# One PSUM tile of two banks for the scores and the up-projections, a quarter of K on GpSimd, and another place for weight splits and the last steps of attention

## The chip, the cores and the metric

The kernel runs on one core of one Trainium2 chip. The metric is the device time of the whole program in microseconds. The engines are called PE (TensorE), DVE (VectorE), ACT (ScalarE), POOL (GpSimd) and SP (SyncE, which issues most transfers). PSUM, the memory that PE writes to, is used here as eight banks of 128 partitions by 512 float32 values.

## The reference

The inputs are `r`, `k`, `v`, `w` of 4 batches, 8 heads, 768 steps and 48 channels, and a mixture of 8 experts (384 to 1024 to 384 channels). First comes a linear attention with a decaying state, then each of the 3072 rows goes through one expert.

```python
for t in range(S):
    cur = np.einsum('bhd,bhe->bhde', u[None] * kt, vt)
    y[:, :, t] = np.einsum('bhd,bhde->bhe', rt, state + cur)
    state = wt[:, :, :, None] * state + np.einsum('bhd,bhe->bhde', kt, vt)
...
logits = x @ w_gate + modality_bias[modality_id]
e_idx = np.argmax(logits, axis=1)
...
for e in range(E):
    h = np.maximum(x[mask] @ w1[e], 0.0)
    out[mask] = gate_w[mask, None] * (h @ w2[e])
```

`gate_w` is the softmax value of the chosen expert.

## The kernel before

The framework runs each engine's instructions in the order in which the code issues them (`manual_schedule`, line 55). It adds the semaphore waits by itself, from which instruction reads and writes which tile. All pools of PSUM have one buffer for a tag, so a tag is a fixed place, and a new tile of a tag waits for the readers of the old one.

**Attention** works on 24 chunks of 128 steps (4 batches of 6 chunks), all heads at once. `att_iter(i)`, for i from -2 to 23, does a third of the work of each of three chunks: it prepares chunk a = i+2, makes scores for m = i+1, and makes the output of z = i.

- Preparing: DVE makes the products of the decays by two scans, `B` (L251) and `E` (L254), and then `R = r*E` (L215) and `K = k*B` (L221). ACT first copies r and k to the PSUM tile `pX` (L211), from which `mk_r` and `mk_k` read. POOL makes `G = r*k` (L256), after the scan `E` by a dependency that the code adds.
- Scores: PE transposes the four 128-wide quarters of K into `pK` (L283), which ACT copies to `KT`, and makes the scores of four head pairs: even heads go to tile `pS0`, odd heads to `pS1`, 512 wide each (L301). DVE multiplies each by the mask into `A` (L303), two operations of 512.
- State: PE adds K^T v into `pU` (L310), ACT scales it to `SP` and copies it into `SPb`.
- Output: PE makes `pY` from R and `SPb` (L331) and from A and v (L337). POOL makes `dV` (L262), the term with `u`; DVE adds the two to `xp` (L361, `x_rows`) one iteration later. One iteration after that PE transposes these rows (L368, `x_cols`), ACT copies them to `xT`, and PE makes the router's logits in the tile `pR` (L374, `logits`).

**Routing** of the first 12 chunks runs inside the loop, as "hooks": `route_a` at i = 14, `route_b` at 15, `table(0)` at 16. All three are mostly small DVE operations. POOL then scatters the rows to their sorted places in DRAM by indirect transfers (L555), two of them at i = 15, three at each of 16 to 18 and one at 19.

**The experts** follow in blocks of 256 rows, 12 of them here, and one half block of 128 rows. Products are made to nearly float32 precision by splitting each operand into a rounded part and a rest: `wh`, `wl` for weights, `xh`, `xo` for rows, `hh`, `hl` for hidden values. A weight split (`w_split`) is a copy on ACT (L206) and a subtraction (L207) on DVE for w1 and on POOL for w2. `blk_up(q, g)` for g = 0 to 3 makes two 128-wide parts of the hidden layer by 18 matmuls (L596) into one PSUM tile of 2 by 256, which takes the tags `pS0`, `pS1`, `pT` in turn. ACT reads it for `hh` (L601), DVE reads it and `hh` for `hl` (L602). `blk_down` (L613) multiplies by w2 into `pY` and `pX`; ACT scales the result and POOL scatters it. `half_up` is the half block's `blk_up`, two groups in `pS0` and `pS1`. In block 0, `x_cols` and `logits` of the last two chunks stand between the groups of `blk_up`, in the tag `pT`.

The first expert's w1 is split during attention, in eight parts of 384 columns, at the iterations that `SPLITS` lists (line 240), on POOL behind `dV`. The bias table of the router is put together early in POOL's queue, with a scratch area `bt2` (line 158) in the space that the raw weights take later.

Of the kernel before, what the change touches and what calls it, by code (L numbers as in the profile page):

```python
# [52 lines left out]
def kernel(ctx: ExitStack, tc: tile.TileContext, rkw, vt, wf, cst, mid, wg, bias, w1, w2, out):  # L53
# [150 lines left out]
    def w_split(k, q, n=2, eng=None):  # L204
        sl = slice(n * q, n * q + n)
        nc.scalar.copy(out=wh[k][:, sl], in_=raw[k][:, sl])  # L206
        (eng or (nc.vector, nc.gpsimd)[k]).tensor_tensor(out=wl[k][:, sl], in0=raw[k][:, sl], in1=wh[k][:, sl].bitcast(F32), op=ALU.subtract)  # L207
# [9 lines left out]
    def mk_k(a):  # L217

        kk = T["pX", a] if a else ins[0][:, 512:1024].rearrange("p (a b) -> p a b", a=4)
        K = wt(a, "K", [P, 4, P])  # L220
        nc.vector.tensor_tensor(out=K, in0=kk, in1=T["B", a][:, 1:517].rearrange("p (a b) -> p a b", a=4)[:, :, 1:129], op=ALU.mult)  # L221
# [20 lines left out]
    def att_iter(i):
# [31 lines left out]
        if ok(m):  # L274
# [23 lines left out]
            for p in range(4):
                for hh in range(2):
                    q = slice(64 * hh, 64 * hh + 64)  # L300
                    nc.tensor.matmul(out=pS[hh][:, p], lhsT=K[q, p], rhs=R[q, p], start=True, stop=True)  # L301
            for hh in range(2):
                nc.vector.tensor_tensor(out=A[:, hh], in0=pS[hh], in1=mask[:, None, :].to_broadcast([P, 4, P]), op=ALU.mult)  # L303
# [20 lines left out]
        if hooks:
            hooks.pop(0)()
        if ok(z):
            A, R, v, pY = T["A", z], T["R", z], T["v", z], pt(z, "pY")
            if not first(z):
                for p in range(4):
                    for q in (0, 64):  # L330
                        nc.tensor.matmul(out=pY[q:q + 64, 2 * p * D:2 * (p + 1) * D], lhsT=R[:, p, q:q + 64],  # L331
                                         rhs=SPb[z % 3][:, p].rearrange("p a b -> p (a b)"),
                                         start=(p == 0), stop=False, skip_group_check=True)
# [628 lines left out]
```

## Time and profile before

| | |
|---|---|
| median of three timed runs | 396.58 us (391.73, 396.58, 398.23) |
| the profiled execution | 392.17 us |
| its span, first to last instruction | 390.3 us |
| mean granted PE clock | 0.965 |
| PE busy | 360.5 us, 92% |
| DVE busy | 246.7 us, 63% |
| ACT busy | 234.1 us, 60% |
| POOL busy | 226.3 us, 58% |

A group of instructions in the profile is named by engine, line, operation and tiles; buffer numbers are left out, so `pS` stands for both `pS0` and `pS1`, and `pT_u` and `pS_u` are the tiles of `blk_up`. The first number in a row of an engine's timeline is the start in us from the span's start, the second the duration. A bracket behind a row gives the idle time of the engine just before it, and who ended it.

### The profile page before, as it was taken

The numbers are of one execution on the slowest core, as the hardware profiler recorded it, in microseconds if no ns is written. First come the engines' busy times: TensorE is split into PE (matmuls) and PEld (weight loads), VectorE is DVE, ScalarE is ACT, GpSimd is POOL, SyncE is SP. The second block draws the span as 40 slices with busy tenths as digits, with TensorE's granted clock in tenths as the row PEclk, the third lists the DMA queues.
The fourth block names the chain that finished last, engine by engine and source line by source line (L and its number), as shares of the span: only waits on it lengthen the run. The fifth ranks groups of instructions, "written<-read, shape, count | busy, mean of one in ns | idle before, by whom it ended". The sixth has DMA issues, their size and how long they took to land.

```text
span 390.3 us, 10893 instructions
## 1 busy us (share of the span) xinstructions
PE 360.5 (92%) x4280; PEld 343.7 (88%) x4280; DVE 246.7 (63%) x407; ACT 234.1 (60%) x480; POOL 226.3 (58%) x194
## 2 busy tenths in 40 slices
PE   5899899998877999999999999999999999999990
PEld 2688888887866988899999999999999999999990
DVE  6899999999998992675265936344261716651010
ACT  2476466668544662667468586777777675854330
POOL 6234643544878742576688895747466474736440
PEclk9589999999996999999999999999999999999996
DMA  7975779999467851001126543131313474166000
GB/s 153 216 159 135 169 187 215 226 235 211 110 162 193 210 187 51 1 3 42 60 103 223 154 171 117 48 122 39 104 43 101 127 260 135 45 208 196 9 28 21
DMA packets 18464, 50.52 MB, mean 129 GB/s; under 512 B 2917, under 2 KB 10635, under 8 KB 18404
## 3 DMA queue, kind: packets, MB, share of 16 engines
q1 hardware_dynamic: 15268, 40.28, 40.5%
q0 software_dynamic: 3136, 9.47, 6.8%
q8 instruction: 35, 0.57, 0.7%
q14 instruction: 25, 0.20, 0.2%
HBM read 72.89 MB, written 11.63 MB: 217 GB/s over the span
## 4 chain that ended last, share of the span: by engine, by line
PE 64%; DVE 18%; issue 10%; ACT 2%; POOL 2%; DMA 2%; SPq 0%; POOLq 0%; DVEq 0%; ACTq 0%
PE pS_u L596 18%; PE pY_d L613 13%; PE pX_d L613 13%; PE pT_u L596 9%; DVE B L251 5%; DVE A L303 4%; DVE K L221 3%; DVE R L215 3%; PE pS L301 3%; DMA in<-rkw 2%; PE pK_x L584 1%; PE pY L337 1%; PE pK L283 1%; PE pY L331 1%; PE pT L368 1%
## 5 line engine op out<-in xcount | busy, mean ns | idle before, releaser
L207 POOL TENSOR_TENSOR wl<-raw,wh 128x768 fp32r<-128x768 f32 (+1 forms) x60 | 104.1, 1743 | 72.9 <-ACT wh L206 72.8
L206 ACT CAST wh<-raw 128x768 fp32r<-128x768 f32 (+1 forms) x104 | 83.4, 805 | 35.1 <-PE pX_d L613 24.9
L256 POOL TENSOR_TENSOR G<-in 128x512 f32<-128x512 f32 x24 | 31.3, 1303 | 58.4 <-PE pS L301 30.6
L602 DVE SCALAR_TENSOR_TENSOR hl<-pS_u,hh 128x512 fp32r<-128x512 f32 x32 | 22.1, 690 | 55.7 <-ACT hh L601 55.7
L211 ACT COPY pX<-in 128x512 f32<-128x512 f32 x47 | 27.7, 590 | 48.1 <-DVE R L215 39.6
L596 PE MATMUL pS_u<-xh,wh 128*128 128x256 f32 x192 | 54.6, 284 | 0.0
L596 PE MATMUL pS_u<-xo,wh 128*128 128x256 f32 x192 | 54.1, 282 | 0.0
L596 PE MATMUL pS_u<-xh,wl 128*128 128x256 f32 x192 | 54.1, 282 | 0.0
L207 DVE TENSOR_TENSOR wl<-raw,wh 128x768 fp32r<-128x768 f32 x44 | 49.4, 1122 | 2.8 <-ACT wh L206 1.8
L621 POOL DMA_INDIRECT out<-ot,xl x25 | 32.5, 1301 | 10.9 <-ACT ot L620 5.3
L596 PEld LDWEIGHTS pS_u<-xo,wh 128*128 128x128 f32 x192 | 36.2, 189 | 0.0
L596 PEld LDWEIGHTS pS_u<-xh,wl 128*128 128x128 f32 x192 | 36.2, 189 | 0.0
L601 ACT ACTIVATE hh<-pS_u 128x512 fp32r<-128x512 f32 x32 | 19.2, 599 | 28.3 <-PE pS_u L596 28.3
L596 PEld LDWEIGHTS pS_u<-xh,wh 128*128 128x128 f32 x192 | 36.0, 188 | 0.1
L602 DVE SCALAR_TENSOR_TENSOR hl<-pT_u,hh 128x512 fp32r<-128x512 f32 x16 | 11.0, 689 | 39.1 <-ACT hh L601 39.1
L613 PE MATMUL pY_d<-wh,hh 128*128 128x384 f32 x96 | 33.5, 349 | 0.0
L303 DVE TENSOR_TENSOR A<-pS,cs 128x512 f32<-128x512 f32 x48 | 30.7, 681 | 4.0 <-PE pS L301 3.9
L251 DVE TENSOR_TENSOR_SCAN B<-in,d1b 128x516 f32<-128x516 f32 x24 | 30.9, 1288 | 3.5 <-DMA in<-rkw 3.5
L613 PE MATMUL pX_d<-wh,hh 128*128 128x384 f32 x96 | 32.5, 338 | 0.0
L613 PE MATMUL pX_d<-wl,hh 128*128 128x384 f32 x96 | 32.4, 338 | 0.0
L613 PE MATMUL pY_d<-wl,hh 128*128 128x384 f32 x96 | 32.4, 338 | 0.0
L613 PE MATMUL pY_d<-wh,hl 128*128 128x384 f32 x96 | 32.4, 338 | 0.0
(187 smaller groups left out, 910.8 us busy)
## 6 DMA issues: line engine op xcount, KB each, us to landing
raw<-w SPq DMA_DIRECT2D x52, 768.0 KB
in<-rkw SPq DMA_DIRECT2D x46, 288.9 KB
xl<-xs SPq DMA_DIRECT2D x12, 386.0 KB
v<-vt SPq DMA_DIRECT2D x24, 192.0 KB
wg<-wf SPq DMA_DIRECT2D x8, 576.0 KB
raw<-w SPq DMA_DIRECT2D x8, 384.0 KB
xs<-zt SPq DMA_DIRECT2D x8, 193.0 KB
out<-ot,xl POOLq DMA_INDIRECT x25, 3.6
```

The source lines that it names most:

```text
L206: nc.scalar.copy(out=wh[k][:, sl], in_=raw[k][:, sl])
L207: (eng or (nc.vector, nc.gpsimd)[k]).tensor_tensor(out=wl[k][:, sl], in0=raw[k][:, sl], in1=wh[k][:, sl].bitcast(F32), op=ALU.subtract)
L211: nc.scalar.copy(out=pt(a, "pX", (P, 4, P)), in_=src.rearrange("p (a b) -> p a b", a=4))
L215: nc.vector.tensor_tensor(out=R, in0=T["pX", a], in1=T["E", a].rearrange("p (a b) -> p a b", a=4)[:, :, 0:P], op=ALU.mult)
L251: nc.vector.tensor_tensor_scan(out=Bt[:, 516:0:-1], data0=w[:, 516:0:-1], data1=d1b[:, 516:0:-1], initial=0.0, op0=ALU.mult, op1=ALU.max)
L256: ins_g = nc.gpsimd.tensor_tensor(out=G, in0=r, in1=k, op=ALU.mult)
L303: nc.vector.tensor_tensor(out=A[:, hh], in0=pS[hh], in1=mask[:, None, :].to_broadcast([P, 4, P]), op=ALU.mult)
L596: nc.tensor.matmul(out=pp[:, i], lhsT=wsrc[0][:, f, c * P:(c + 1) * P], rhs=xsrc[:, c], start=(n == 0), stop=(n == 3 * KC - 1))
L601: nc.scalar.activation(out=hh, in_=pp, func=AF.Relu)
L602: nc.vector.scalar_tensor_tensor(out=hl, in0=pp, scalar=0.0, in1=hh.bitcast(F32), op0=ALU.max, op1=ALU.subtract)
L613: nc.tensor.matmul(out=X["y", q][j], lhsT=hsrc[:, i, j * P:(j + 1) * P], rhs=wsrc[1][:, f], start=(f == 0 and n == 0), stop=(f == FC - 1 a ...
L621: ins = nc.gpsimd.indirect_dma_start(out=out[:, :], out_offset=bass.IndirectOffsetOnAxis(ap=xl[:, j, DM + 1:DM + 2].bitcast(I32), axis=0), ...
```

## The change

There are six edits.

1. The scores of all heads go into one tile `pS` of two banks, and one masking operation of 1024 takes the place of two of 512.
2. `mk_k3` makes the last quarter of K on POOL, from the input in SBUF, right behind `dV`. ACT copies and DVE multiplies the other three quarters.
3. The first expert's w1 is split in halves of 192 columns: four at i = 14, one at 15, four at 16, three at 22, and the last four behind the loop.
4. `x_rows(16)` moves from iteration 17 to the end of iteration 16, behind the table. In iteration 22, `x_cols(20)` moves behind the scores, and `logits(20)` and `x_cols(21)` are put between the two parts of `pY`; the latter uses the tag `pK`. In iteration 23, `logits(21)` stands behind `pY`.
5. `bt2` lies in another part of the raw weights' space.
6. `blk_up` and `half_up` take their two `pS` places as two views of one tile, made once (`up_bank`). In block 0 the groups use these two views in turn; from block 1 on, each third group uses `pT`, as before.

```diff
-    bt2 = raw[0][:, 0, 0:NU * E].rearrange("p (a e) -> p a e", a=NU)
+    bt2 = raw[1][:, FC - 1, 0:NU * E].rearrange("p (a e) -> p a e", a=NU)
...
+    def w_split_half(n):
+        f, c = n // 2, n % 2 * (DM // 2)
+        part = lambda t: t[:, f, c:c + DM // 2]
+        nc.scalar.copy(out=part(wh[0]), in_=part(raw[0]))
+        nc.gpsimd.tensor_tensor(out=part(wl[0]), in0=part(raw[0]), in1=part(wh[0]).bitcast(F32), op=ALU.subtract)
...
+    def rk_psum(a, src, n=4):
+        nc.scalar.copy(out=pt(a, "pX", (P, 4, P))[:, 0:n], in_=src.rearrange("p (a b) -> p a b", a=4)[:, 0:n])
...
     def mk_k(a):
 
-        kk = T["pX", a] if a else ins[0][:, 512:1024].rearrange("p (a b) -> p a b", a=4)
+        n = 3 if a else 4
+        kk = T["pX", a] if a else quarters(ins[0][:, 512:1024])
+        nc.vector.tensor_tensor(out=T["K", a][:, 0:n], in0=kk[:, 0:n], in1=quarters(T["B", a][:, 1:517])[:, 0:n, 1:129], op=ALU.mult)
+
+    def mk_k3(a, k):
         K = wt(a, "K", [P, 4, P])
-        nc.vector.tensor_tensor(out=K, in0=kk, in1=T["B", a][:, 1:517].rearrange("p (a b) -> p a b", a=4)[:, :, 1:129], op=ALU.mult)
+        if a:
+            nc.gpsimd.tensor_tensor(out=K[:, 3], in0=quarters(k)[:, 3], in1=quarters(T["B", a][:, 1:517])[:, 3, 1:129], op=ALU.mult)
...
-    SPLITS = (10, 11, 12, 13, 14, 14, 16, 22)
+    SPLITS = {14: 4, 15: 1, 16: 4, 22: 3}
...
-        for _ in range(SPLITS.count(i)):
-            w_split(0, next(done), 1, nc.gpsimd)
-        if ok(z - 1):
+        if ok(a):
+            mk_k3(a, k)
+        for _ in range(SPLITS.get(i, 0)):
+            w_split_half(next(done))
+        if ok(z - 1) and i != NJ + 5:
             x_rows(z - 1)
...
-            if ok(z - 2):
+            if ok(z - 2) and i < NU - 2:
                 x_cols(z - 2, pT)
...
             if ok(a):
-                rk_psum(a, k)
+                rk_psum(a, k, 3)
             A = wt(m, "A", [P, 2, 4, P])
-            pS = [pt(m, f"pS{hh}", (P, 4, P)) for hh in range(2)]
+            pS = pt(m, "pS", (P, 2, 4, P))
             for p in range(4):
                 for hh in range(2):
                     q = slice(64 * hh, 64 * hh + 64)
-                    nc.tensor.matmul(out=pS[hh][:, p], lhsT=K[q, p], rhs=R[q, p], start=True, stop=True)
-            for hh in range(2):
-                nc.vector.tensor_tensor(out=A[:, hh], in0=pS[hh], in1=mask[:, None, :].to_broadcast([P, 4, P]), op=ALU.mult)
+                    nc.tensor.matmul(out=pS[:, hh, p], lhsT=K[q, p], rhs=R[q, p], start=True, stop=True)
+            if i == NU - 2:
+                x_cols(z - 2, pT)
+            nc.vector.tensor_tensor(out=A.rearrange("p a b c -> p (a b) c"), in0=pS.rearrange("p a b c -> p (a b) c"),
+                                    in1=mask[:, None, :].to_broadcast([P, H, P]), op=ALU.mult)
...
-        elif ok(z - 2):
-            x_cols(z - 2, pt(m, "pT"))
-        if ok(z - 2):
+        if ok(z - 2) and i < NU - 2:
             logits(z - 2)
...
+            if i == NU - 2:
+
+                logits(z - 2)
+                x_cols(z - 1, pt(m + 1, "pK"))
...
+        if i == NU - 1:
+            logits(z - 2)
+        if i == NJ + 4:
+
+            x_rows(z)
...
+    def up_bank(n):
+
+        if "up" not in X:
+            X["up"] = pt("up", "pS", (P, 2, 2, BT))
+        return X["up"][:, n]
+
     def blk_up(q, g):
         xh, xo = X["x", q]
-        pp = pt(f"u{q}_{g}", ("pS0", "pS1", "pT")[(q * (FC // 2) + g) % 3] if isinstance(q, int) else f"pS{g % 2}", (P, 2, BT))
+        n = (q * (FC // 2) + g) % 3 if isinstance(q, int) and q else g % 2
+        pp = pt(f"u{q}_{g}", "pT", (P, 2, BT)) if n == 2 else up_bank(n)
...
-        pp = pt(f"u{q}_{k}", f"pS{k}", (P, FC // 2, P))
+        pp = up_bank(k).rearrange("p a (b c) -> p (a b) c", c=P)
...
         att_iter(i)
+        if i == NU - 1:
+            for n in done:
+                w_split_half(n)
```

The built programs differ as follows at three places. A row names the line, the operation, the tiles with the program's buffer numbers, and the shape; in brackets stand the semaphores of the engines or transfer queues that it waits for.

On PE, at the start of block 0, from the end of the first group of `blk_up` to the start of the second, with the transposes of `x_cols` between. Before:

```order
L596 MATMUL pS_u_0_2824<-xo_2741,wh_68 128x256
L596 MATMUL pS_u_0_2824<-xh_2740,wl_69 128x256
L368 MATMUL pT_('x', 0)_2848<-cs,xp_1592 128x128 [waits PE_49]
L368 MATMUL pT_('x', 0)_2848<-cs,xp_1592 128x128 x2
L596 MATMUL pS_u_1_2858<-xh_2740,wh_68 128x256
```

And now:

```order
L628 MATMUL pS_up<-xo_2730,wh_68 128x256
L628 MATMUL pS_up<-xh_2729,wl_69 128x256
L393 MATMUL pT_('x', 0)_2839<-cs,xp_1572 128x128 [waits PE_49]
L393 MATMUL pT_('x', 0)_2839<-cs,xp_1572 128x128 x2
L628 MATMUL pS_up<-xh_2729,wh_68 128x256 [waits DVE_49]
```

The order is the same. The second group's first matmul, which had no wait, now waits for a DVE instruction: the `hl` of the first group.

On ACT, in block 2, the `hh` of the four groups with the weight copies between them. Before:

```order
L601 ACTIVATE hh_0_3323<-pT_u_0_3304 128x512 [waits PE_49]
L206 CAST wh_68<-raw_66 128x768 [waits DMAHW7_49,DVE_49]
L601 ACTIVATE hh_1_3351<-pS_u_1_3332 128x512 [waits PE_49]
L206 CAST wh_68<-raw_66 128x768 [waits DVE_49]
L601 ACTIVATE hh_2_3379<-pS_u_2_3360 128x512 [waits PE_49]
L206 CAST wh_68<-raw_66 128x768 [waits DMAHW0_49,DVE_49]
L601 ACTIVATE hh_3_3407<-pT_u_3_3388 128x512 [waits PE_49]
```

And now:

```order
L633 ACTIVATE hh_0_3308<-pT_u_0_3289 128x512 [waits PE_49]
L206 CAST wh_68<-raw_66 128x768 [waits DMAHW7_49,Activation_49]
L633 ACTIVATE hh_1_3335<-pS_up 128x512 [waits DVE_49,PE_49]
L206 CAST wh_68<-raw_66 128x768 [waits Activation_49]
L633 ACTIVATE hh_2_3362<-pS_up 128x512 [waits DVE_49,PE_49]
L206 CAST wh_68<-raw_66 128x768 [waits DMAHW0_49,Activation_49]
L633 ACTIVATE hh_3_3390<-pT_u_3_3371 128x512 [waits PE_49]
```

The order is the same again. The two groups in the shared tile have a wait for DVE more.

On POOL, in iteration 16 and the start of 17, from one `G` to behind the next `dV`, with the scatters (DMA) between. Before:

```order
L256 TENSOR_TENSOR G_1951<-in_85 128x512 [waits DMAHW4_49,DMAHW5_49,DVE_49,PE_49]
L262 TENSOR_TENSOR dV_1953<-v_1684,dT_1932 128x384 [waits DMAHW7_49,Activation_49]
L207 TENSOR_TENSOR wl_69<-raw_66,wh_68 128x384 [waits DMAHW2_49,Activation_49]
L555 DMA xs<-xp_351,posT 26880x386 x3
L256 TENSOR_TENSOR G_2064<-in_86 128x512 [waits DMAHW0_49,DVE_49,DMAHW7_49,PE_49,Pool_49]
L262 TENSOR_TENSOR dV_2066<-v_1805,dT_2042 128x384 [waits DMAHW3_49,Activation_49]
```

And now:

```order
L270 TENSOR_TENSOR G_1932<-in_85 128x512 [waits DMAHW4_49,DMAHW5_49,DVE_49,PE_49]
L276 TENSOR_TENSOR dV_1934<-v_1661,dT_1913 128x384 [waits DMAHW7_49,Activation_49]
L232 TENSOR_TENSOR K_1936<-in_85,B_1925 128x128
L213 TENSOR_TENSOR wl_69<-raw_66,wh_68 128x192 [waits Activation_49] x3
L213 TENSOR_TENSOR wl_69<-raw_66,wh_68 128x192 [waits DMAHW6_49,Activation_49]
L580 DMA xs<-xp_351,posT 26880x386 x3
L270 TENSOR_TENSOR G_2051<-in_86 128x512 [waits DMAHW0_49,DVE_49,DMAHW7_49,PE_49,Pool_49]
L276 TENSOR_TENSOR dV_2053<-v_1785,dT_2029 128x384 [waits DMAHW3_49,Activation_49]
L232 TENSOR_TENSOR K_2055<-in_86,B_2044 128x128 [waits Pool_49]
```

The quarter of K stands behind `dV`, and four halves of a split stand where one whole part stood, ahead of the three scatters.

More of the change, by code (lines that the diff above doesn't have):

```diff
@@ L202, in w_raw, with w_split @@
                           in_=(w1, w2)[k][ds(e, 1), :, part * n * DM:(part + 1) * n * DM].rearrange("a p c -> (a p) c"), **kw)
-    def w_split(k, q, n=2, eng=None):
+    def w_split(k, q, n=2):
         sl = slice(n * q, n * q + n)
         nc.scalar.copy(out=wh[k][:, sl], in_=raw[k][:, sl])
-        (eng or (nc.vector, nc.gpsimd)[k]).tensor_tensor(out=wl[k][:, sl], in0=raw[k][:, sl], in1=wh[k][:, sl].bitcast(F32), op=ALU.subtract)
-    def rk_psum(a, src):
-        nc.scalar.copy(out=pt(a, "pX", (P, 4, P)), in_=src.rearrange("p (a b) -> p a b", a=4))
+        (nc.vector, nc.gpsimd)[k].tensor_tensor(out=wl[k][:, sl], in0=raw[k][:, sl], in1=wh[k][:, sl].bitcast(F32), op=ALU.subtract)
+    def w_split_half(n):
[5 more added lines that the diff above has]
+        nc.scalar.copy(out=pt(a, "pX", (P, 4, P))[:, 0:n], in_=src.rearrange("p (a b) -> p a b", a=4)[:, 0:n])
     def mk_r(a):
@@ L217, in mk_k, with quarters @@
     def mk_k(a):
-        kk = T["pX", a] if a else ins[0][:, 512:1024].rearrange("p (a b) -> p a b", a=4)
+        n = 3 if a else 4
+        kk = T["pX", a] if a else quarters(ins[0][:, 512:1024])
+        nc.vector.tensor_tensor(out=T["K", a][:, 0:n], in0=kk[:, 0:n], in1=quarters(T["B", a][:, 1:517])[:, 0:n, 1:129], op=ALU.mult)
+    def mk_k3(a, k):
         K = wt(a, "K", [P, 4, P])
-        nc.vector.tensor_tensor(out=K, in0=kk, in1=T["B", a][:, 1:517].rearrange("p (a b) -> p a b", a=4)[:, :, 1:129], op=ALU.mult)
+        if a:
+            nc.gpsimd.tensor_tensor(out=K[:, 3], in0=quarters(k)[:, 3], in1=quarters(T["B", a][:, 1:517])[:, 3, 1:129], op=ALU.mult)
+    def quarters(v):
+        return v.rearrange("p (a b) -> p a b", a=4)
     def first(n):
@@ L237 @@
     hooks = []
-    done = iter(range(FC))
-    SPLITS = (10, 11, 12, 13, 14, 14, 16, 22)
+    done = iter(range(2 * FC))
+    SPLITS = {14: 4, 15: 1, 16: 4, 22: 3}
     def att_iter(i):
@@ L873, in any_decay @@
                     nc.sync.dma_start(out=xl, in_=xd[ds(n * P, P), :])
-                    px, pl, ph, py = pt("gx", "pT"), pt("gl", "pR"), pt("gh", "pS0"), pt("gy", "pY")
+                    px, pl, ph, py = pt("gx", "pT"), pt("gl", "pR"), up_bank(0).rearrange("p a b -> p (a b)"), pt("gy", "pY")
                     for c in range(KC):
```

## Prediction

> **What bounds the kernel now.** I read the page's first two parts, then the busy time of two stretches, then who waited for whom, then single engines in order of time.
>
> ```profile
> span 390.3 us, 10893 instructions
> 0.00:152.00 152.00, 133.25 (x2593) 117.60 (x2593) 138.91 (x228) 87.39 (x251) 82.81 (x100) 0.93 0.77 181
> 152.00:380.00 228.00, 226.82 (x1686) 226.04 (x1687) 107.81 (x180) 146.11 (x230) 142.50 (x93) 1.00 0.31 100
> PE pR_x L374 <- ACT xT L369: 0.8, 1, 0.8
> PE pT_u L596 <- ACT xT L369: 0.7, 1, 0.7
> ```
>
> Columns of a stretch: length, then busy PE, weight load, VectorE (DVE), ScalarE (ACT), GpSimd (POOL), clock. There are two regimes. In attention (to 152) VectorE is busy 138.91 of 152. In the expert blocks (152 to 380) TensorE is busy 226.82 of 228 at full clock; the two waits listed, 1.5 us together, are all that TensorE has from 152 to the end. So attention's price is VectorE's, the blocks' price is any wait of TensorE.
>
> One attention iteration on VectorE, and what TensorE needs for one:
>
> ```profile
> 55.21 1.22 DVE L251 TENSOR_TENSOR_SCAN B<-in,d1b 128x516 f32<-128x516 f32 x1
> ...
> 57.83 0.53 DVE L361 TENSOR_TENSOR xp<-pY,dV 128x384 f32<-128x384 f32 x1
> 58.28 0.68 DVE L215 TENSOR_TENSOR R<-pX,E 128x512 f32<-128x512 f32 x1
> 58.88 1.28 DVE L303 TENSOR_TENSOR A<-pS,cs 128x512 f32<-128x512 f32 x2
> 60.07 0.68 DVE L221 TENSOR_TENSOR K<-pX,B 128x512 f32<-128x512 f32 x1
> 60.67 1.22 DVE L251 TENSOR_TENSOR_SCAN B<-in,d1b 128x516 f32<-128x516 f32 x1
> 129.76 0.66 PE L283 MATMUL pK<-cs,K 128*128 128x128 f32 x4
> ...
> 135.07 0.66 PE L283 MATMUL pK<-cs,K 128*128 128x128 f32 x4
> ```
>
> Starts follow each other without idle time: the two maskings take 60.07-58.88 = 1.19, K 0.60, xp 58.28-57.83 = 0.45, the whole iteration (B to B) 5.46. TensorE, when late, does one in 135.07-129.76 = 5.31, only 0.15 less; but the first and last chunk of a sequence leave matmuls out, so over six chunks VectorE stays the bound.
>
> **The change part by part.** *VectorE in attention.*
>
> ```profile
> 116.39 0.15 DVE L490 TENSOR_SCALAR tabe<-pR_x 128x5 f32<-128x5 f32 x1
> 116.46 0.15 DVE L491 TENSOR_SCALAR tab<-pR_x 128x5 int32<-128x5 f32 x1
> L251 DVE TENSOR_TENSOR_SCAN B<-in,d1b 128x516 f32<-128x516 f32 x24 | 30.9, 1288 | 3.5 <-DMA in<-rkw 3.5
> ```
>
> Five elements cost 0.07 from start to start, 512 cost 0.60: 1.045 ns an element. One masking of 1024 is then 0.07+1.065 = 1.135, a saving of 0.055 (bounds 0 and 0.07, one small operation). K at 384 wide costs what xp costs, 0.45: 0.15 saved. Together 0.205 in 22 iterations (24 chunks, less both ends), **-4.5** (bounds -3.3, -4.8). The scan B takes 1.22 alone, 1.288 in the mean over 24: 24 x 0.065 = 1.5 us, lost mainly beside the weight splits that leave iterations 10 to 13: **-1.5**.
>
> *K's last quarter on GpSimd.*
>
> ```profile
> 58.05 1.31 POOL L256 TENSOR_TENSOR G<-in 128x512 f32<-128x512 f32 x1 [2.84 <-PE pS L301]
> 59.31 0.83 POOL L262 TENSOR_TENSOR dV<-v,dT 128x384 f32<-128x384 f32 x1
> 43.90 0.52 POOL L175 TENSOR_TENSOR biasT<-m,bb 128x192 f32<-128x192 f32 x1
> 81.73 0.83 POOL L262 TENSOR_TENSOR dV<-v,dT 128x384 f32<-128x384 f32 x1
> 82.52 1.00 POOL L207 TENSOR_TENSOR wl<-raw,wh 128x384 fp32r<-128x384 f32 x1
> 83.03 1.58 DVE L251 TENSOR_TENSOR_SCAN B<-in,d1b 128x516 f32<-128x516 f32 x1
> 49.15 0.51 POOL L175 TENSOR_TENSOR raw<-m,bb 128x192 f32<-128x192 f32 x1
> 49.74 1.22 DVE L251 TENSOR_TENSOR_SCAN B<-in,d1b 128x516 f32<-128x516 f32 x1
> ```
>
> A scan that meets a split waits: 83.03+1.58-1.22 = 83.39, that is 0.13 before the split's end (83.52). The quarter (128 wide, estimate 0.45 from 0.52 at 192 and 1.00 at 384) would start 0.79 after dV (as the split at 82.52 does), at 60.10, and let the scan go at 60.42; the scan is due at 60.67-0.205 = 60.465. Cost 0, by 0.04 only; were it 0.1 longer, 22 x 0.06 = +1.3. The Trainium skill's page "SBUF — State Buffer", section "SBUF: two separate sides", says that a VectorE operation with two SBUF inputs and a GpSimd operation take the shared ports for a whole instruction, and the other blocks: it speaks against this edit, and by it the sum would stand at +1.3 here, not 0, wherever the quarter is late. The row at 83.03 bears the rule out. Setup work behind the quarter moves 0.41 later into a scan (49.15 against 49.74; likewise in two or three more iterations): **+0.8** (0 to 1.6).
>
> *Routing (iterations 14 to 19).*
>
> ```profile
> 119.28 0.53 DVE L361 TENSOR_TENSOR xp<-pY,dV 128x384 f32<-128x384 f32 x1
> 119.87 0.88 PE L331 MATMUL pY<-SPb,R 128*64 128x96 f32 x16 [2.46 <-DVE xp L361]
> 121.00:122.00 1.00, 1.00 (x24) 1.00 (x23) 1.00 (x3) 0.97 (x6) 0.84 (x2) 0.50 0.14 35
> 127.49 1.29 DVE L303 TENSOR_TENSOR A<-pS,cs 128x512 f32<-128x512 f32 x2 [1.62 <-PE pS L301]
> 121.83 1.01 POOL L555 DMA_INDIRECT xs<-xp,posT  x1 [0.16 <-DVE A L303]
> 123.14 0.98 POOL L555 DMA_INDIRECT xs<-xp,posT  x1 [0.30 <-issue]
> ```
>
> x_rows(16) now stands ahead of the two scans, so TensorE's 2.46 wait goes; behind it the clock fell to 0.50 and VectorE waited 1.62 for the scores. But GpSimd gets two more split halves' worth and a quarter in front of three scatters of 1.31 each, and TensorE's transposes now wait for that quarter. Gain up to 1.6, loss up to 3: I take **0**, for the two mechanisms are of one size.
>
> *The end of attention.* S stands ahead of the transposes, logits(21) behind pY:
>
> ```profile
> 146.39 0.55 PE L368 MATMUL pT<-cs,xp 128*128 128x128 f32 x3 [0.52 <-ACT dT L235]
> 152.45 0.52 PE L374 MATMUL pR_x<-cs,xT 128*64 128x8 f32 x12 [0.79 <-ACT xT L369]
> 154.53 0.39 PE L596 MATMUL pS_u<-xh,wh 128*128 128x256 f32 x1
> ```
>
> Both waits are TensorE's in front of the first block (its first matmul at 154.53), 0.52+0.79: **-1.3** (0 to -1.5). The last four halves run on GpSimd behind attention, 4 x 0.52, and block 0's fourth group needs them three groups later: 0. The bias table's new place frees the first weight load a little sooner: 0, no load is waited for there.
>
> *The blocks.* Before, groups of blk_up rotate over three PSUM tiles; now two of the three are banks of one tile. In the built program TensorE's first matmul into one bank waits for the `hl` (L634) of the group just before, though that reads the other bank: once in each of blocks 1 to 11, three times in block 0, once in the half block. Before, such waits looked two groups back. What is exposed:
>
> ```profile
> 177.38 0.28 PE L596 MATMUL pT_u<-xh,wh 128*128 128x256 f32 x1
> 177.50 0.29 PE L596 MATMUL pT_u<-xo,wh 128*128 128x256 f32 x1
> 177.58 0.60 ACT L601 ACTIVATE hh<-pS_u 128x512 fp32r<-128x512 f32 x1 [0.32 <-PE pS_u L596]
> 178.21 0.69 DVE L602 SCALAR_TENSOR_TENSOR hl<-pS_u,hh 128x512 fp32r<-128x512 f32 x1 [3.30 <-ACT hh L601]
> ...
> 160.48 0.39 PE L596 MATMUL pT_u<-xh,wh 128*128 128x256 f32 x1 [0.73 <-ACT xT L369]
> 160.70 0.28 PE L596 MATMUL pT_u<-xo,wh 128*128 128x256 f32 x1
> 161.33 0.68 DVE L602 SCALAR_TENSOR_TENSOR hl<-pS_u,hh 128x512 fp32r<-128x512 f32 x1
> ```
>
> The next group started at 177.38; it would wait until 178.21+0.69 = 178.90, plus 0.06 to take the release (xp ended 119.81, TensorE began 119.87): 1.58. Restarting costs 0.10 (the second matmul 0.22 behind the first, against 0.12). So 1.68 a stall; nothing gives it back, for TensorE has no other wait there. Eleven blocks: **+18.5** (each 1.5 without the restart, 1.85 where hl is queued). The half block's two groups: **+1.6** (1.4 to 1.8). Block 0: three stalls, 5.0, less 1.2 for the transposes and logits that stand between (an estimate, by 0.55 and 0.52 above), less the 0.7 wait at 160.48 which goes with pT, plus 0.7 because hl is late there: 161.33+0.68+0.06 = 162.07 is 2.32 after 159.75, where that group could have started without its 0.73 wait, against 1.58: **+3.8** (2.5 to 4.5).
>
> A page that would have it otherwise is "PSUM — Partial Sum Buffer", section "PSUM bank collisions raise a hardware error": engines on different banks do not collide, so guard by bank. By it none of these waits is needed and the sum would lose the 23.9. But the program has the waits, and the chip follows the program; no run shown here tests the banks.
>
> **Sum.** 18.5+1.6+3.8-4.5-1.5+0.8-1.3 = +17.4. The profiled execution took 392.17 (span 390.3 and 1.87 around it): 409.6. The three timed runs were 391.73, 396.58, 398.23, median 4.4 above it; I add half of that: **411.8**.
>
> **The rivals.** *No stall:* the evacuation is over when the next group starts, or only the same bank is awaited. Then 392.2-6.5 = 385.7 in the profile, about 388 timed: not slower. The place is the boundary of two groups, the price 1.68, and it decides when a stall costs under 6.5/15 = 0.43. For it: TensorE never waited before. Against: before, the next group's bank had been free for two groups, and hh and hl alone last 1.29. 5%.
>
> *GpSimd as the bound of iterations 16 to 19:* each scatter holds 1.31, three of them, G, dV and the quarter make about 6.5 against VectorE's 5.3; backlog passes through the quarter to the transposes, S and A. Price up to 3 above my 0, with scans blocked on top: 414.8. For it: no gap of GpSimd in its rows at 121.83 and 123.14 but issue. Against: only the fourth of the transposes needs the quarter, and S comes later still. 13%.
>
> *The clock falls at the stalls:* if a wait of 1.6 lets the clock drop as the 2.46 one did, a group (18 matmuls of 0.12, 2.16) takes twice that, 15 times: about +32, 444. Against it: the waits of 0.79 and 0.73 left the clock at 1.00 in the mean from 152 on. 2%. The page "TensorE: Matmul & The Clock Gate", section "Why this matters for your kernels", asks for gaps of over about 3 us; by that it would not fall. The row at 121 fell after 2.46 beside slack work, so the row does not agree to the letter.
>
> **How the numbers follow.** My forecast 80%, no stall 5%, GpSimd 13%, clock 2%. With all costs at their low ends (+20.4 in the blocks, -9.4 before) the profile is 403.2; at the high ends (+26.7, +1.1) 420. Timed runs may lie a few us above their profile, so the range is 404 to 420. A difference of 2%, 7.9 us, is about what measurement tells from none: bounds 388.6 and 404.5. Slower takes the forecast but for its low end, GpSimd and the clock: 0.91; within, the rest of the low end and part of no stall: 0.06; faster 0.03.
>
> **What would show it.** TensorE should list 15 waits of blk_up's pS_up on hl, 1.5 to 1.7 each, in the blocks, and pT groups without one; the 226.8 of 228 falls to about 90%. VectorE's K should last 0.53, one A about 1.2, the iteration 5.25. Scans of 1.58 should be gone from iterations 10 to 13. Wrong would be: no such waits, or the first block starting no earlier than before (154.5).

## The result, and the profile after

The changed kernel takes 417.21 us in the median of four runs (415.58 to 418.74), the kernel before 395.69 (391.73 to 398.23). The ratio is 1.057, with a 95% interval of 1.051 to 1.063: slower. Ratios here and below compare fast runs with fast runs, so they need not be the quotient of the two medians beside them. The forecast was 411.8, slower, with a range of 404 to 420. The profiled execution took 416.68 us; its span is 414.7 us, 24.4 more than before.

Where the 24.4 lie is read from one moment, the first matmul of the first block. First the busy time from there to the end, in the changed kernel (columns as in the prediction: length, PE, weight load, DVE, ACT, POOL, clock):

```profile
155.00:414.70 259.70, 229.02 (x1629) 224.78 (x1627) 107.07 (x178) 145.92 (x229) 142.07 (x97) 0.99 0.27 89
158.00:404.00 246.00, 225.54 (x1603) 221.86 (x1604) 107.07 (x178) 144.81 (x228) 139.83 (x93) 1.00 0.29 93
```

The same stretch of the kernel before:

```profile
154.50:390.30 235.80, 225.17 (x1631) 224.09 (x1627) 107.01 (x178) 146.29 (x229) 143.47 (x94) 0.99 0.30 98
```

The blocks are 23.9 longer with nearly the same number of matmul records (1629 and 1631) and the same clock. Attention ends 0.5 later. So the blocks cost what was forecast, and attention's forecast gain of 6.5 is missing. The waits of PE from 145 on, in the changed kernel (total, times, longest):

```profile
PE pS_up L628 <- DVE hl L634: 17.9, 15, 1.4
PE pS_up L628 <- issue: 1.4, 1, 1.4
PE pS_up L679 <- DVE hl L684: 1.4, 1, 1.4
```

Before, this list had three waits of 2.0 together. Now there are 17, 20.7 us in all: two of them are 0.2 and 0.3 long, the other 15 are the expected ones, 1.0 to 1.2 in block 0 and 1.41 in the later blocks. One of these on PE, and what DVE did there, in the order of time (start, duration):

```profile
184.95 0.28 PE L628 MATMUL pS_up<-xh,wl 128*128 128x256 f32 x1
186.64 0.39 PE L628 MATMUL pS_up<-xh,wh 128*128 128x256 f32 x1 [1.41 <-DVE hl L634]
186.86 0.28 PE L628 MATMUL pS_up<-xo,wh 128*128 128x256 f32 x1
```

```profile
185.90 0.69 DVE L634 SCALAR_TENSOR_TENSOR hl<-pS_up,hh 128x512 fp32r<-128x512 f32 x1 [0.47 <-ACT hh L633]
```

`hl` of the group before ends at 186.59 and the next group starts at 186.64. From the last matmul of one group to the first of the next are 1.69, where 0.12 is the rule; the second follows 0.22 later in place of 0.12. That is 1.67 for a stall; the prediction had 1.68.

In attention, a quiet iteration of DVE now, from scan B to scan B:

```profile
75.92 1.22 DVE L265 TENSOR_TENSOR_SCAN B<-in,d1b 128x516 f32<-128x516 f32 x1
...
79.59 1.22 DVE L320 TENSOR_TENSOR A<-pS,cs 128x1024 f32<-128x1024 f32 x1
80.72 0.55 DVE L227 TENSOR_TENSOR K<-pX,B 128x384 f32<-128x384 f32 x1
81.19 1.22 DVE L265 TENSOR_TENSOR_SCAN B<-in,d1b 128x516 f32<-128x516 f32 x1
```

It takes 5.27 in place of 5.46. The masking takes 80.72 - 79.59 = 1.13 (1.19 before), K takes 0.47 (0.60). By iteration 15 scan B starts at 98.93, before the change at 102.45: a gain of 3.5, although a load of the second chunk came 0.9 late in this execution. By iteration 21 the gain is gone (140.76 against 140.22). It is lost where POOL scatters. POOL there, from one `G` to the next, in the changed kernel:

```profile
117.45 1.30 POOL L270 TENSOR_TENSOR G<-in 128x512 f32<-128x512 f32 x1
118.69 0.84 POOL L276 TENSOR_TENSOR dV<-v,dT 128x384 f32<-128x384 f32 x1
119.48 1.35 POOL L232 TENSOR_TENSOR K<-in,B 128x128 f32<-128x128 f32 x1
121.00 1.94 POOL L580 DMA_INDIRECT xs<-xp,posT  x1 [0.16 <-issue]
123.23 0.97 POOL L580 DMA_INDIRECT xs<-xp,posT  x1 [0.30 <-issue]
124.51 0.97 POOL L580 DMA_INDIRECT xs<-xp,posT  x1 [0.30 <-issue]
125.50 1.30 POOL L270 TENSOR_TENSOR G<-in 128x512 f32<-128x512 f32 x1
126.73 0.85 POOL L276 TENSOR_TENSOR dV<-v,dT 128x384 f32<-128x384 f32 x1
```

And DVE beside it:

```profile
118.96 1.67 DVE L265 TENSOR_TENSOR_SCAN B<-in,d1b 128x516 f32<-128x516 f32 x1
...
124.70 1.22 DVE L320 TENSOR_TENSOR A<-pS,cs 128x1024 f32<-128x1024 f32 x1 [1.54 <-PE pS L317]
125.84 0.55 DVE L227 TENSOR_TENSOR K<-pX,B 128x384 f32<-128x384 f32 x1
126.31 2.37 DVE L265 TENSOR_TENSOR_SCAN B<-in,d1b 128x516 f32<-128x516 f32 x1
```

POOL has no idle time but the short ones at issue, and one round takes 8.05; DVE's iterations there take 7.35 and 8.38. Scan B takes 1.67 and 2.37 in place of 1.22. It waits for `dV`: the scan alone would have started at 118.96 + 1.67 - 1.22 = 119.41, which is 0.12 before `dV` ends at 119.53, and the next one at 127.46, 0.12 before the next `dV` ends at 127.58. K's quarter, 0.41 in quiet iterations, takes 1.35, because it waits for the scan: it ends 0.2 after it. PE then waits for the quarter (0.82 at 120.89), and DVE for the scores.

### The profile page after: what moved, and what is told of

Its sections match the earlier page's. It is cut to its first block, busy times and chain, and to the rows that moved or that the text cites. A ratio compares the mean times of both kernels' runs of the same rounds, so it can differ in the third digit from the quotient of the medians.

```text
span 414.7 us, 10939 instructions
## 1 busy us (share of the span) xinstructions
PE 368.1 (89%) x4280; PEld 345.8 (83%) x4280; DVE 244.8 (59%) x383; ACT 232.3 (56%) x488; POOL 242.3 (58%) x225
## 4 chain that ended last, share of the span: by engine, by line
PE 58%; DVE 20%; issue 11%; POOL 4%; ACT 3%; DMA 2%; SPq 0%; POOLq 0%; DVEq 0%; ACTq 0%
PE pS_up L628 16%; PE pY_d L645 12%; PE pX_d L645 12%; PE pT_u L628 7%; DVE B L265 5%; DVE A L320 3%; DVE R L221 2%; DVE hl L634 2%; PE pS L317 2%; DVE K L227 2%; ACT hh L633 2%; DMA in<-rkw 2%; PE pY L357 2%; PE pK_x L609 1%; PE pK L299 1%
## 5 line engine op out<-in xcount | busy, mean ns | idle before, releaser
L207 POOL TENSOR_TENSOR wl<-raw,wh 128x768 fp32r<-128x768 f32 x52 | 96.0, 1853 | 93.7 <-ACT wh L206 93.0
L206 ACT CAST wh<-raw 128x768 fp32r<-128x768 f32 x96 | 79.3, 830 | 35.1 <-PE pX_d L645 23.2
L628 PE MATMUL pS_up<-xh,wh 128*128 128x256 f32 x198 | 57.6, 291 | 19.3 <-DVE hl L634 17.9
L628 PEld LDWEIGHTS pS_up<-xh,wh 128*128 128x128 f32 x198 | 37.2, 188 | 22.6 <-DVE hl L634 21.0
L628 PE MATMUL pS_up<-xh,wl 128*128 128x256 f32 x198 | 55.8, 282 | 0.0
L628 PE MATMUL pS_up<-xo,wh 128*128 128x256 f32 x198 | 55.7, 281 | 0.0
L217 ACT COPY pX<-in 128x512 f32<-128x512 f32 (+1 forms) x47 | 25.3, 538 | 47.3 <-DVE R L221 37.9
L628 PEld LDWEIGHTS pS_up<-xo,wh 128*128 128x128 f32 x198 | 37.4, 189 | 0.0
L628 PEld LDWEIGHTS pS_up<-xh,wl 128*128 128x128 f32 x198 | 37.2, 188 | 0.0
L645 PE MATMUL pX_d<-wh,hl 128*128 128x384 f32 x96 | 32.4, 337 | 0.0
```

What stands on the lines that cost most here:

```text
L207: (nc.vector, nc.gpsimd)[k].tensor_tensor(out=wl[k][:, sl], in0=raw[k][:, sl], in1=wh[k][:, sl].bitcast(F32), op=ALU.subtract)
L217: nc.scalar.copy(out=pt(a, "pX", (P, 4, P))[:, 0:n], in_=src.rearrange("p (a b) -> p a b", a=4)[:, 0:n])
L628: nc.tensor.matmul(out=pp[:, i], lhsT=wsrc[0][:, f, c * P:(c + 1) * P], rhs=xsrc[:, c], start=(n == 0), stop=(n == 3 * KC - 1))
L645: nc.tensor.matmul(out=X["y", q][j], lhsT=hsrc[:, i, j * P:(j + 1) * P], rhs=wsrc[1][:, f], start=(f == 0 and n == 0), stop=(f == FC - 1 a ...
```

## The experiments

The theory after this reading has two parts: each wait on the `hl` of the group just before costs 1.68, because two banks are one tile; and attention's gain is lost to POOL's queue beside routing. The first four runs below were made on one chip beside the kernel before, and so were the next four and the last four; the three chips are different ones, and only the kernel before ran on all three (medians of 392.11, 391.78 and 395.63). A place in time, such as the start of the first block, is read from one profiled execution of each run.

### Two tiles for the blocks

Only the blocks are changed: the tile of two banks lies in a pool that closes with attention, and two tiles take its place.

```diff
+    pools = {"pS": att.enter_context(tc.tile_pool(name="pss", bufs=1, space=bass.MemoryType.PSUM))}
...
-        if "up" not in X:
-            X["up"] = pt("up", "pS", (P, 2, 2, BT))
-        return X["up"][:, n]
+        X["ups"] = X.get("ups", 0) + 1
+        return pt(f"up{X['ups']}", f"pS{n}", (P, 2, BT))
...
     att.close()
+    pools["pS0"] = pools["pS1"] = ctx.enter_context(tc.tile_pool(name="psu", bufs=1, space=bass.MemoryType.PSUM))
```

> The changed kernel with one edit undone: behind attention the two places of the up-projections are again two tiles (tags of their own), and the tile of two banks belongs to attention alone. Theory (each wait on the hl of the group just before costs 1.68): the waits of PE on hl in front of a first matmul go, the stretch from the first block's first matmul to the end falls from 259.7 to about 235.8, the profiled time from 416.7 to about 393, no more than 1% from the kernel before. Rival (the blocks are slower for another reason, such as two banks next to each other or the splits that now end behind attention): the stretch stays above 250 and the time above 407.

Measured: 390.8 us, ratio to the kernel before 0.997 (0.993 to 1.002). From the first block on:

```profile
155.60:390.50 234.90, 224.97 (x1631) 224.09 (x1627) 107.01 (x178) 146.22 (x229) 145.50 (x97) 0.98 0.30 98
```

The stretch fell from 259.7 to 234.9, and no wait of PE is left in it. The rival falls. Five of the six edits together, without the stalls, are worth nothing that can be measured: attention ends at 155.6, as late as in the changed kernel.

### The one tile kept, another order of groups

```diff
-        n = (q * (FC // 2) + g) % 3 if isinstance(q, int) and q else g % 2
+        n = g % 4 // 2 if g % 2 == 0 else 2
...
-        pp = up_bank(k).rearrange("p a (b c) -> p (a b) c", c=P)
+        pp = pt(f"u{q}_{k}", "pT", (P, FC // 2, P)) if k else up_bank(k).rearrange("p a (b c) -> p (a b) c", c=P)
...
-                    x_cols(NU - 2 + g, pt(("x", g), "pT"))
+                    x_cols(NU - 2 + g, pt(("x", g), "pX"))
```

> The changed kernel with the one tile of two banks kept, but the groups of the up-projections go to it only every second time and to pT in between (x_cols of block 0 takes the tag pX). Theory (it is the group just before that is waited for, not the layout of two banks): no group waits for the hl of the group before it, blocks as in the run with two tiles, 235.8 to 238, time 392 to 396. Rival (a tile of two banks is slow to use by itself, whoever comes before): a wait stays at each second group and the time stays above 405.

Measured: 392.23 us, ratio 1.000 (0.997 to 1.003). The waits of PE from 145 on:

```profile
PE pT_u L628 <- DVE hl L634: 0.6, 1, 0.6
PE pS_up L628 <- DVE hl L634: 0.2, 1, 0.2
```

The first block starts at 154.27 and the span ends at 390.4, so the blocks take 236.1. Two banks in one tile cost nothing by themselves; the cost comes when two groups that follow each other use the same tile.

### Only the one tile and the one masking, on the kernel before

This is the kernel before with edits 1 and 6. Its core:

```diff
-            pS = [pt(m, f"pS{hh}", (P, 4, P)) for hh in range(2)]
+            pS = pt(m, "pS", (P, 2, 4, P))
...
+        n = (q * (FC // 2) + g) % 3 if isinstance(q, int) and q else g % 2
+        pp = pt(f"u{q}_{g}", "pT", (P, 2, BT)) if n == 2 else up_bank(n)
```

> The kernel before with edits 1 and 6 alone: one tile of two banks for the scores, one masking operation, and the same tile for the up-projections. Theory: attention gains 22 times 0.055, 1.2; the blocks lose the whole 23.9; profiled time about 415, ratio to before 1.055 to 1.06. Rival (the loss needs the new order of splits and x_cols at the end as well): the blocks lose less than 18, ratio under 1.045.

Measured: 414.26 us, ratio 1.054 (1.048 to 1.061). The blocks:

```profile
153.50:412.60 259.10, 228.84 (x1631) 224.81 (x1627) 106.74 (x178) 146.28 (x229) 142.16 (x94) 0.99 0.27 89
```

And the waits of PE from 145 on that come from `hl`:

```profile
PE pS_up L602 <- DVE hl L608: 18.9, 15, 1.4
PE pS_up L653 <- DVE hl L658: 1.4, 1, 1.4
```

They lose 259.1 - 235.8 = 23.3, a little less than expected, as is the ratio. The whole loss comes with these two edits. Attention ends 1.0 earlier, at 153.51; the masking's 1.2 was expected.

### No quarter of K on POOL beside routing

As the run with two tiles, and in iterations 14 to 19 DVE makes all of K.

```diff
+    def nq(a):
+        return 4 if a == 0 or 14 <= a - 2 <= 19 else 3
```

`nq(a)` stands in `mk_k`, in the condition of `mk_k3` and in ACT's copy in place of 3.

> As the run with two tiles, and the last quarter of K is made by DVE again in iterations 14 to 19, where POOL scatters. Theory (POOL is the bound there: G, dV, K's quarter and three scatters make 8.0 an iteration, the quarter's 1.35 being mostly a wait for a scan): iterations 17 to 19 fall to 6.0 to 6.6, first block's start moves from 155.0 to about 151.5, time 3 to 4 below the run with two tiles, although six K cost 0.15 more each. Rival (the scatters and the split halves alone hold POOL, or PE bounds these iterations): start of the first block within 1 of 155, time the same or 0.9 more.

Measured: 387.91 us, ratio 0.987 (0.981 to 0.993). One round of POOL with three scatters:

```profile
116.77 1.28 POOL L274 TENSOR_TENSOR G<-in 128x512 f32<-128x512 f32 x1
118.00 0.84 POOL L280 TENSOR_TENSOR dV<-v,dT 128x384 f32<-128x384 f32 x1
119.00 1.75 POOL L584 DMA_INDIRECT xs<-xp,posT  x1 [0.16 <-issue]
121.05 1.15 POOL L584 DMA_INDIRECT xs<-xp,posT  x1 [0.30 <-issue]
122.51 0.98 POOL L584 DMA_INDIRECT xs<-xp,posT  x1 [0.30 <-issue]
123.49 1.30 POOL L274 TENSOR_TENSOR G<-in 128x512 f32<-128x512 f32 x1
```

The first block's first matmul, on PE:

```profile
151.45 0.39 PE L631 MATMUL pS_up<-xh,wh 128*128 128x256 f32 x1
```

A round takes 6.72 in place of 8.05, and the first block starts at 151.45, 4.2 earlier than with two tiles alone. The medians differ by less, 2.9, for the profiled execution with two tiles (392.36) was 1.6 over its median. So those six quarters cost 3 to 4; sixteen in quiet iterations bring 0.13 each, 2.1. POOL still has no slack in this round.

### Two quarters of K on POOL

As the run before, but POOL makes two quarters where it made one, and DVE the other two.

```diff
-        return 4 if a == 0 or 14 <= a - 2 <= 19 else 3
+        return 4 if a == 0 or 14 <= a - 2 <= 19 else 2
...
+            nc.gpsimd.tensor_tensor(out=K[:, 2:4], in0=quarters(k)[:, 2:4], in1=quarters(T["B", a][:, 1:517])[:, 2:4, 1:129], op=ALU.mult)
```

> As the run with no K on POOL beside routing, but POOL makes two quarters of K in the other iterations, and DVE only the other two (0.13 less an iteration on DVE). Theory (the quarter of 0.37 is just in time, and whatever POOL does longer holds the scan B back, for both use the same memory port): POOL takes about 0.35 longer, DVE is ready 0.13 earlier, so the scan B lasts 1.6 to 1.75 in place of 1.22, and the quiet iterations rise from 5.27 to 5.55 to 5.65. Rival (POOL and the scan run side by side, and DVE's work alone sets the iteration): 5.13 to 5.15, B stays at 1.22.

Measured, in a single execution: 390.66 us. DVE and POOL in a quiet iteration:

```profile
76.55 1.62 DVE L269 TENSOR_TENSOR_SCAN B<-in,d1b 128x516 f32<-128x516 f32 x1
...
82.08 1.59 DVE L269 TENSOR_TENSOR_SCAN B<-in,d1b 128x516 f32<-128x516 f32 x1
```

```profile
76.39 0.69 POOL L233 TENSOR_TENSOR K<-in,B 128x256 f32<-128x256 f32 x1
```

DVE has 0.14 less work, and the iteration is 0.26 longer: 5.53. POOL ends at 77.08 and the scan at 78.17, 1.09 later; a scan alone takes 1.22, so the scan ran from 0.13 before POOL's end, as the prediction had read it. The rival, both side by side, asked for 5.13 and falls. The size is a little under the 5.55 to 5.65 expected.

### The end and `x_rows(16)` as before

Two runs on top of the one without K beside routing, which itself was made on the chip of the first four. In the first, `x_cols` and `logits` of iterations 22 and 23 stand where they stood before the change.

```diff
-            if ok(z - 2) and i < NU - 2:
+            if ok(z - 2):
                 x_cols(z - 2, pT)
...
-            if i == NU - 2:
-
-                logits(z - 2)
-                x_cols(z - 1, pt(m + 1, "pK"))
...
```

> As the run with no K on POOL beside routing, with the old order at the end: x_cols and logits of the last three chunks in iterations 22 and 23 where they were. The prediction's term for the new order was 1.3. Theory A (that term holds): from the start of scan B of iteration 21 to the first block rises from 14.0 by 0.8 to 1.5, time 1 more. Theory B, which the trace of the changed kernel speaks for (14.24 there against 14.31 before: the two waits went and others of VectorE and TensorE came in their place): within 0.4 of 14.0, time the same.

Measured: 389.29 us, ratio 0.993 (0.990 to 0.996). From scan B of iteration 21 to the first block: 137.25 to 152.24, 14.99, where the new order takes 137.44 to 151.45, 14.01. Theory A holds in this pair: the new order is worth 1.0, and the medians differ by 1.4. In the changed kernel the same stretch took 14.2 and before the change 14.3, so there the gain does not show. The pair is weak evidence by itself: with the same new order the stretch is 13.2 to 15.3 in eight of the other runs here and 17.0 in a ninth. The runs do not show what moves it.

In the second, `x_rows(16)` is back in iteration 17.

```diff
-        if ok(z - 1) and i != NJ + 5:
+        if ok(z - 1):
             x_rows(z - 1)
...
-        if i == NJ + 4:
-
-            x_rows(z)
```

> As the run with no K on POOL beside routing, with x_rows(16) back in iteration 17, behind the scans. Theory A (the early x_rows(16) takes TensorE's 2.46 wait away, up to 1.6 for the end of attention): the wait of pY for xp comes back at about 2.4, first block 1 to 1.6 later than 151.45. Theory B (POOL with its scatters bounds iterations 16 to 19 anyway, 6.5 to 6.7 each, so TensorE's wait is hidden behind that): the wait comes back, first block within 0.5 of 151.45.

Measured: 387.45 us, ratio 0.986 (0.978 to 0.995). The wait that the edit had taken away is back in the list of waits:

```profile
PE pY L351 <- DVE xp L387: 2.9, 2, 2.5
```

And the first block starts earlier all the same, not later:

```profile
150.56 0.39 PE L628 MATMUL pS_up<-xh,wh 128*128 128x256 f32 x1
```

That is 0.9 before 151.45, of which 0.3 was there already at iteration 16. Theory A falls, and theory B's 0.5 is missed on the other side. A wait of PE of 2.5 was removed and bought nothing: the run with the early `x_rows(16)` has another one soon behind that place, which ends at 118.65 and is not in this run's list:

```profile
PE pK L303 <- DVE K L228: 3.0, 1, 3.0
```

### The splits where they were

Again on top of the run without K beside routing: the halves stand at the iterations of the kernel before.

```diff
-    SPLITS = {14: 4, 15: 1, 16: 4, 22: 3}
+    SPLITS = {10: 2, 11: 2, 12: 2, 13: 2, 14: 4, 16: 2, 22: 2}
```

> As the run with no K on POOL beside routing, with the weight splits (in halves) at the iterations of the kernel before: 10 to 14, 16 and 22. Theory: iterations 10 to 13 rise from 5.27 to 6.0 to 6.2, since two halves behind K's quarter hold the next scan B back by 0.8 to 0.9 each; iterations 14 to 16 lose no more halves of 15 and two of 16, 0.5 to 1.1 less; nothing hangs on halves behind attention. In sum the first block 2 to 3 later than 151.45. Rival (POOL's queue at 14 to 16 is what counts): the first block no later than 152.

Measured: 385.93 us, ratio 0.982 (0.975 to 0.988). The first block starts at 149.19, 2.3 earlier; the theory, 2 to 3 later, was wrong, and the rival's bound, 152, holds. The gain does not lie beside the splits: scan B of iteration 15 starts at 98.69, without the edit at 98.61. It comes after iteration 19, and the clock differs there too, 1.00 from 120 to 130 in place of 0.53 and 0.50. The runs do not show what brought it. POOL and DVE in one of the iterations with two halves:

```profile
80.33 0.40 POOL L233 TENSOR_TENSOR K<-in,B 128x128 f32<-128x128 f32 x1
80.69 1.51 POOL L214 TENSOR_TENSOR wl<-raw,wh 128x192 fp32r<-128x192 f32 x1
82.17 1.52 POOL L214 TENSOR_TENSOR wl<-raw,wh 128x192 fp32r<-128x192 f32 x1
```

```profile
80.52 1.31 DVE L269 TENSOR_TENSOR_SCAN B<-in,d1b 128x516 f32<-128x516 f32 x1
81.86 0.18 DVE L271 RECIPROCAL d1e<-B 128x4 f32<-128x4 f32 x1
82.07 1.23 DVE L272 TENSOR_TENSOR_SCAN E<-in,d1e 128x516 f32<-128x516 f32 x1
85.86 1.32 DVE L269 TENSOR_TENSOR_SCAN B<-in,d1b 128x516 f32<-128x516 f32 x1
```

The iteration takes 5.34, only 0.07 over a quiet one. Scan B is 0.1 longer, held by K's quarter. The halves take 1.5 each in place of about 0.5: each ends 0.4 after a scan does. Here POOL waits for the scan, which had started before it. Before the change a whole part stood directly behind `dV`, ran already when the scan came, and held it back by 0.36.

### Fewer scatters at a time, and no K on POOL

Four runs, all on the one with the old places of the splits and beside one another, on a chip on which the kernel before took 395.63. First two scatters in each of iterations 15 to 20.

```diff
-        drain(2 if i == NJ + 3 else 3)
+        drain(2)
```

> As the run with the old places of the splits, and two scatters in each of iterations 15 to 20 where there were two, three, three, three and one in 15 to 19. Theory (POOL's queue is the bound where three scatters stand: G, dV and three of 1.31 make about 6.5): iterations of 6.6 go, all are about 5.45, first block 0.5 to 1.1 earlier than 149.19, time 0.5 to 1 lower. Rival (a scatter that meets a scan costs the same wherever it stands): the wait moves to iteration 20, first block within 0.3.

Measured: 388.65 us, ratio 0.985 (0.980 to 0.991). First block at 152.68: 3.5 later in the profile, against the theory. What PE waited for from 95 on:

```profile
PE pT L397 <- ACT dT L253: 2.4, 2, 1.6
PE pY L361 <- issue: 1.6, 4, 0.4
```

Neither wait was in the run with three scatters in this size (0.8 for `dT`, none for issue). POOL's rounds are still long, 6.9, 6.0 and 6.3 from 121.34 on, but it is no longer busy through them: 2.65 of the 5 us from 125 to 130, with three scatters 4.38. So its queue is not what makes these rounds long; other waits have come. The rival, within 0.3, falls too. (The run with three scatters was made on the chip of the four runs before, so the 3.5 lies across two chips.) The gaps of 0.4 within the matmuls of `pY` are there in the changed kernel too, at 115.8 to 118.0; no run shows their cause.

With `x_rows(16)` back as well, by the same lines as above:

> As the run with two scatters, and x_rows(16) back in iteration 17. Theory A (without POOL's backlog TensorE's wait of 2.4 shows): VectorE waits 1.6 for scores behind it, first block 1 to 1.6 later than with two scatters. Theory B (the early x_rows(16) brings nothing here either): within 0.5.

Measured: 389.46 us, ratio 0.989 (0.983 to 0.995), first block at 152.83: no difference to the run above, theory B.

With no K on POOL at all, and three scatters again:

```diff
-        return 4 if a == 0 or 14 <= a - 2 <= 19 else 3
+        return 4
```

> As the run with the old places of the splits, with no quarter of K on POOL at all. Theory (the quarter is worth what DVE saves, 0.13 to 0.15 an iteration): quiet iterations rise from 5.27 to 5.40 to 5.42, 16 of them, first block 2.0 to 2.5 later than 149.19, time 2 higher. Rival (the quarter's lock on the scans eats its gain): first block within 0.7 of 149.19.

Measured: 389.2 us, ratio 0.987 (0.980 to 0.993). Quiet iterations take 5.40, as expected: 0.13 is what a quarter brings. On the total this run says little: three of its six times are 387.4 to 387.6 and three 390.8 to 391.8. The profile is of the longer kind, with a wait of PE of 3.1 for `dT` in iteration 19 and the first block at 154.81.

This run also shows what cutting a split in halves does by itself, for here the halves stand directly behind `dV`, where the whole part stood before the change:

```profile
75.95 0.60 POOL L214 TENSOR_TENSOR wl<-raw,wh 128x192 fp32r<-128x192 f32 x1
76.37 1.26 DVE L269 TENSOR_TENSOR_SCAN B<-in,d1b 128x516 f32<-128x516 f32 x1
```

The first half is ahead of the scan, but ends at 76.55, and the scan loses 0.04 and not 0.36. The second half then waits for the scan.

With two scatters and the quarter in all iterations:

```diff
-        return 4 if a == 0 or 14 <= a - 2 <= 19 else 3
+        return 3 if a else 4
```

> As the run with two scatters, and K's quarter on POOL in all iterations. If POOL has room with two scatters (G, dV, quarter and two of 1.31 make 5.1 against 5.27 on DVE): six iterations gain 0.13 each, first block up to 0.8 earlier than with two scatters. If the waits for scans, which the quarter and a scatter share, take that room: iterations 17 to 20 rise to 6 to 7, first block 1 to 4 later.

Measured: 388.92 us, ratio 0.986 (0.981 to 0.992), first block at 151.42. Iterations 17 to 20 take 5.0 to 5.9, so the second expectation falls. A scan of 2.73 in iteration 21, a wait of PE of 2.4 for DVE's K and two for POOL's quarter, 1.6 together, are new against the run with two scatters; the first block is 1.3 earlier in the profile, and the times do not differ. Whether POOL has room for the quarter then stays open.

The lowest ratio is that of the version with two tiles in the blocks, the splits at their old places in halves, and K's quarter on POOL away from routing only: 0.982 (0.975 to 0.988), on its own chip, where the medians are 385.93 and 391.78. The four later variants lie between 0.985 and 0.989, with intervals that overlap its own, so no run shows that it is better than they are.

## Why the prediction was right, and where it was not

**The blocks.** The mechanism and the size were right. Forecast were 15 stalls of 1.68 and +23.9 in all; measured are 15 waits of that kind, 1.67 from matmul to matmul in a later block, and +23.9. In block 0 the waits were 1.13, 1.22 and 0.96. The waits that the profile lists, 1.41, look shorter than the 1.5 to 1.7 that were to show, because idle time is counted from a modelled end. The rule of the page "PSUM — Partial Sum Buffer" of the Trainium skill, section "PSUM bank collisions raise a hardware error", to guard by bank, would have asked for no wait here. The runs bear the rule out and not its use as a forecast: with two tiles PE writes one bank while DVE reads the other and 24.8 us go away (259.7 to 234.9), but the program of the changed kernel had the waits.

**DVE in attention, -4.5.** Right in the mechanism: 0.19 an iteration against 0.205, the masking 0.06, the quarter 0.13.

**The scans beside the splits, -1.5.** Here a step failed. Iterations 11 to 14 did lose the longer scans. But the splits' new places cost more than that: put back, in halves, the first block starts 2.3 earlier; by what is open. And the move was not needed for the gain. The prediction had charged the scan's 0.36 to the split's place. It belongs to a whole part that is still running when the scan comes: a half in the same place costs it 0.04, and of two halves behind the quarter it feels only the quarter, 0.1.

**K's quarter, 0 to +0.8.** Right in quiet iterations: scan B stays at 1.22, so the margin of 0.04 held. Of the +0.8 for the setup work the changed kernel shows 0.44 (scan B at 54.43 takes 1.66) and 0.2 (scan E at 45.14 takes 1.44), against one loss of 0.13 before: about 0.5. The two quarters show the mechanism, and agree with the page "SBUF — State Buffer", section "SBUF: two separate sides", of the Trainium skill, that one operation waits for the whole of the other (here up to 0.13 before its recorded end): the iteration is 0.26 longer with 0.14 less work.

**Routing, 0.** This step failed most. "Gain up to 1.6, loss up to 3, I take 0": between iterations 15 and 21 the change lost 4.1, more than the bound. The rival named GpSimd as the bound of iterations 16 to 19 and got 13% as a case apart; it came true on top of the forecast, and its 414.8 lies nearer to the measured 417.2 than the forecast's 411.8. Its sum of POOL's work, 6.5, left out that the quarter and the first scatter also wait for scans: 8.05 was measured. The quarter is the part that does it (without it 4.2 less in the profile, 2.9 in the medians). The gain that was set against it, TensorE's wait, was no gain.

**The end, -1.3.** It measured 1.0 in the pair of runs that tests it, and 0.1 in the changed kernel, where the two waits went and others came. So the term is of the right size in one pair and brought nothing in the changed kernel.

**The sum.** +23.9 was right and -6.5 came out at +0.5, so the profile of 409.6 became 416.68. The 2.2 for the spread of the timed runs was too much: the timed median lies 0.5 over the profile. That the result lies inside the range rests on the range's high end, which had the losses in attention in it: the blocks came out at their middle, attention at +0.5 of a highest +1.1. For attention that is luck, since its terms were not right one by one.

**The clock.** No stall lowered it: it is 1.00 from 158 to 404, with waits of 1.41 in it. This agrees with the page "TensorE: Matmul & The Clock Gate", section "Why this matters for your kernels", of the Trainium skill, that asks for longer gaps. In attention it fell to 0.50 between 120 and 130 in the changed kernel:

```profile
120.00:125.00 5.00, 4.18 (x31) 3.46 (x32) 3.39 (x6) 1.87 (x4) 4.23 (x4) 0.50 0.79 178
125.00:130.00 5.00, 5.00 (x80) 4.99 (x77) 4.93 (x5) 2.45 (x9) 4.82 (x5) 0.50 0.43 141
```

Before, it was 0.57 and 0.74 there. Here the trace does not agree with that page: from 112 until the clock had fallen, at 120, no idle time of PE was longer than 0.5. But PE was busy for only 1.24 of the 3 us from 115 to 118, shortly ahead of the fall:

```profile
115.00:118.00 3.00, 1.24 (x19) 0.76 (x13) 2.83 (x5) 0.52 (x2) 2.55 (x3) 1.00 0.68 163
```

What part of routing's 4.1 is the clock's and what the queue's, the runs do not separate: without the quarter the clock fell there too (0.53 and 0.50), and the first block still started 4.2 earlier.

## What to carry to other kernels

A wait is as coarse as the tile that it guards: whoever joins two buffers into one tile, for one cheap wide operation, should look at who reuses that tile right after, and read the built program for waits that look one step back where they looked two. A saving of 0.2 an iteration is worth nothing if the engine that takes the work is the bound in a few iterations; count its queue there, with the waits that it shares with others. And where operations of two engines hold each other up, look at what is still running when the other engine comes: here a split cost the scan 0.36 in one piece and 0.04 in halves at the same place.

## What was not expected of the hardware

Two halves of a split behind K's quarter cost DVE 0.07 an iteration, although POOL is busy with them for 3.0; the same work in one piece, directly behind `dV`, cost 0.36 to 0.4. Who came first does not always go first: a scan that comes while `G` runs waits not only for `G` but for the `dV` behind it as well, though `dV` starts later than the scan came. So it is at 126.31 in the changed kernel (2.37 in place of 1.22), and in the runs without K's quarter beside routing, at 124.11 (2.56) and 129.42 (2.56). A scan that came while K's quarter ran, at 80.52, went ahead of the half behind it. No run shows what makes the difference. And the kernel is uneven where PE has little to do: in the fastest version the clock is 0.50 from 110 to 115 and 0.76 from 115 to 120, and 1.00 behind that; in the changed kernel it is down from 120 to 130. What sets the place of the drop, and how much of the 2 to 4 us by which these versions differ in routing is its, stays open.
